# Two gated weight conversions more, a third fetch buffer and a second set of sum tiles in an attention plus two-MLP kernel

## The chip, the cores and the metric

The kernel runs on one core of a Trainium2 chip. The metric is the device time of one execution in microseconds (us), as the median of several runs.

## The reference

All data are float32; the weights reach the kernel as float64 and are narrowed on the chip.

```python
# attention: q, k, v of (4 batches, 12 heads, 448 rows, 64)
scores = cap * tanh((q @ k.T / 8) / cap)          # cap is 30
x = softmax(scores) @ v                           # heads side by side: 1792 x 768
h = x @ w_in                                      # first MLP, 768 x 2048
x = (h - tanh(h)) @ w_out                         # 2048 x 768
h = x @ w_in2                                     # second MLP, same shapes
out = (h * 1 / (1 + exp(-1.702 * h))) @ w_out2    # 1792 x 768
```

## The kernel before

The kernel runs in two phases. Attention goes through 24 groups `g` (a batch and a pair of heads). For each group TensorE makes transposes, scores and products with v; ScalarE (ACT) does tanh (L519) and exp (L521) on score tiles of 128x896; VectorE (DVE) does sums and copies. The order of these instructions is written by hand: `pin` keeps an instruction in program order on its engine. Everything that is not pinned is placed by a planner, which orders each engine's instructions by priority and by its own estimate of when their inputs are ready. Each engine then executes its list in the order so fixed.

The MLPs use TensorE with pairs of tiles: each operand is split in a rounded part and a rest (`hi_act` on ACT, L81; `lo_dve` on DVE, L93), and three products are added. The tokens are cut in two passes of 768 and 1024. The first layer's up projection (`gemm_in(0)`, product line L869) and its down projection for the first 768 tokens (`gemm_out`, L909) come first. Then come, for the 1024 tokens, `gemm_in(0)` again, the down projection in seven products instead of eight (`gemm_out_seven`, L962), the second up projection in seven products (`gemm_in_seven`, L1047) and the second down projection (`gemm_rows_seven`, L1149), and the last two again for the 768 tokens. `gemm_in_seven` makes 8 rounds `j` of 7 products, each 9 matmuls of 512 columns for the 1024 tokens.

Weights come in 64 chunks of 128x768. Chunks 0 to 15 are the first up projection, 16 to 31 the first down projection (A0 and up), 32 to 47 the second up projection (I0 and up), 48 to 63 the second down projection (R0 and up). A chunk is converted by `convert`: `conv_exp` on ACT (L193), `conv_low` on ACT (L200) or DVE (L202), `conv_or` on DVE (L208), and for chunks under 32 the split of L81 and L93. `conv_low` multiplies the low words in place in the landed tile `wd`; it needs nothing but the transfer. The transfer is issued by `dbl_dma` (L179) on the SP queue, called at the end of the `conv_or` of an earlier chunk. `wd` has two buffers (`wd_p`). A third (`some["wd"]`, opened at L1257 after attention in the program) is used where the running number of the transfer is divisible by three. `order` says which chunk has which number: nine "early" chunks (0, 1, 2, 4, 6, 8, 10, 12, 14) are numbers 0 to 8 and are converted inside the attention by hand; 3, 5, 7, 9, 11, 13, 15 are numbers 9 to 15, and `prepare` converts them in the loop of the first up projection. There `prepare` opens `tc.issue_after` for each instruction in `marks`: an instruction traced inside the block, if it is on the mark's engine, is placed behind the mark. `marks` holds the last exp of the attention (ACT) and the last reciprocal (DVE).

In the later stages, converted chunks lie in DRAM and `fetch` brings them back to `wr_p` (two buffers, tile `whole`), on the SP queue too; `third`, where it is not empty, is one more buffer for every third number, and makes `prepare` fetch two chunks ahead instead of one (L306). Side work runs beside the products: `sums_a`, `sums_i` (chunks 32 to 47) and `sums_b` (chunks 48 to 63, in four groups of four chunks, `group`) are generators, and `beside` takes a step of the first one each time that `due` has grown by one; it grows by `rate` at each call, which is once a chunk in the two seven-product stages concerned. `sums_b` takes six steps a group. `until("b")` ends it ahead of the second down projection.

Of the kernel before, what the change touches and what calls it, by code (L numbers as in the profile page):

```python
# [9 lines left out]
F32 = mybir.dt.float32  # L10
# [18 lines left out]
LEAD = 2  # L29
# [11 lines left out]
def attention_moe_moe(ctx, tc, q, k, v, cap, w_in1, w_out1, w_in2, w_out2, out):  # L41
# [3 lines left out]
    P = 128  # L45
# [6 lines left out]
    KF = DF // P  # L52
# [3 lines left out]
    WC = KM * P  # L56
    HW = DM // 2
    NT = max(TOKENS)
# [100 lines left out]
    early = [0, 1, 2, 4, 6, 8, 10, 12, 14]  # L159
    A0, I0, R0 = KF, 2 * KF, 3 * KF  # L160
    KQ = KF // 4
# [4 lines left out]
    n_raw, third, group, side_p, made = [0], [], [], [], [-1]  # L166
    n_dbl, n_ready, n_use = [0], [0], [0]
# [29 lines left out]
    def conv_low(i, act=False):  # L197
        low = dbls[i][:, :, 0]
        if act:
            pin(nc.scalar.mul(out=low, in_=low, mul=F64_LOW))  # L200
        else:
            pin(nc.vector.tensor_scalar(  # L202
                out=low, in0=dbls[i].bitcast(U16)[:, :, 1], scalar1=F64_LOW * 2.0 ** 16, scalar2=None, op0=ALU.mult
            ))
# [27 lines left out]

    def convert(i):
        conv_exp(i)
        conv_low(i, n_use[0] < KF or i >= I0)
        conv_or(i)
        if i < I0:
            conv_hi(i)
            conv_lo(i)
            n_ready[0] += 1  # L240

    KH = KF // 2
    SEVEN_A = ("11", "12", "s2", "s1", "s3", "s4", "22")
# [14 lines left out]
    W0 = len(stream)  # L258
# [25 lines left out]
    def prepare(upto):  # L284
        while n_ready[0] <= min(upto, len(stream) - 1):
            i = n_ready[0]
            if i < I0 and i not in early:
                with ExitStack() as behind:
                    if i < 2 * LEAD + 2:
                        for ins in marks:  # L290
                            behind.enter_context(tc.issue_after(ins))
                    convert(i)
                continue
            whl[i] = tuple(wh_p.tile([P, WC], F32R, tag=tag, name=tag) for tag in ("wh", "wl"))
            src, n, _ = stream[i]
            fetch(i)
            if i in whole:
                x = whole.pop(i)
                h, l = (t[:, :n] for t in whl[i])
                with tc.high_priority(offset=150):  # L300
                    hi_act(h, x)
                    lo_dve(l, x, h)
            else:
                for m, t in enumerate(whl[i]):
                    nc.sync.dma_start(out=t[:, :n].bitcast(F32), in_=src[:, m])
            for n in range(1, 2 + len(third)):  # L306
                fetch(i + n)
            n_ready[0] += 1
# [10 lines left out]
    side, due, rate = [], [0.0], [1.0]  # L319
# [18 lines left out]
    def add(out, a, kind, b):  # L338
        nc.vector.tensor_tensor(out=out, in0=a, in1=b, op=kind)
# [50 lines left out]

    def sums_b():
        for j in range(KQ):
            group[:] = [side_p[0].tile([P, WC], F32, tag="wr", name="group") for _ in range(2)]
            group.append(g_p.tile([P, NT], F32, tag="t", name="group")[:, :WC])
            group.extend(spare)
            for n in range(4):
                i = R0 + n * KQ + j
                convert(i)
                raws.pop(i)
                yield  # L400
            r11, r21, r12, r22 = group
            sub(r22, r22, r12)
            sub(r12, r12, r11)
            for m, t in (("t3", r22), ("t1", r12)):
                nc.sync.dma_start(out=side_b[m][j], in_=t)
            yield
            add(r11, r22, ALU.add, r11)
            sub(r21, r21, r11)
            for m, t in (("t2", r11), ("t4", r21)):
                nc.sync.dma_start(out=side_b[m][j], in_=t)  # L410
            yield
        done.add("b")
# [388 lines left out]
    gr, spare, ring, last_ts = [], [], [], []  # L801
# [134 lines left out]
    def gemm_out_seven():  # L936
        def three():
            return [one_bank("ps_y")[:, :HT] for _ in range(3)]

        def temps(*tags):  # L940
            return [part_of(t) for t in tags]

        LO, HI = slice(0, HT), slice(HT, NT)
        banks = {}
        p1 = u2 = None
        p5 = [gr[2 + e][:, HT:] for e in range(3)]
        for p, name in enumerate(SEVEN_A):
            rate[0] = .4 if p < 5 else 0.0
            head = {"12": "12", "s1": "s1", "s4": "s1"}.get(name, "11")
            if name == head:  # L950
                banks[head] = three()
            ps = banks[head]
            for j in range(KQ):
                i, (wh, wl) = w_next()
                ahead(i)
                for e in range(3):
                    c = slice(e * P, (e + 1) * P)
                    for kk in range(2):
                        k = 2 * j + kk
                        h, l = ring[k]  # L960
                        for m, (w, x) in enumerate(((wh, h), (wh, l), (wl, h))):
                            nc.tensor.matmul(  # L962
                                ps[e], w[:, kk, c], x,
                                start=(name == head and k == 0 and m == 0), stop=(k == KH - 1 and m == 2), skip_group_check=True,
                            )
                for k in (2 * j, 2 * j + 1):
                    if p < 6:
                        right(p + 1, k)
                    elif k in (3, 6):
                        for e in range(3):  # L970
                            split(ring[k - 3 + e], (p5 if k == 3 else u2)[e])
                if p == 0 and j == 0:
                    run_late()
            if p == 0:
                p1 = temps("far", "far", "v")
            elif p == 2:
                u2 = temps("q", "q", "t")
            with tc.high_priority(offset=AHEAD):
                for e in range(3):
                    if name == "11":  # L980
                        nc.scalar.copy(out=p1[e], in_=ps[e])
                    elif name == "12":
                        add(p1[e], ps[e], ALU.add, p1[e])
                    elif name == "s2":
                        nc.scalar.copy(out=u2[e], in_=ps[e])
                    elif name == "s1":
                        nc.scalar.copy(out=p5[e], in_=ps[e])
                    elif name == "s3":
                        add(p5[e], ps[e], ALU.add, p5[e])
                    elif name == "s4":  # L990
                        add(u2[e], ps[e], ALU.add, u2[e])
                    else:
                        x_out(3 + e, LO, ps[e])
            for e in range(3):
                if name == "12":
                    x_out(e, LO, p1[e])
                elif name == "s3":
                    x_out(3 + e, HI, p5[e])
                elif name == "s4":
                    sub(p1[e], u2[e], p1[e])  # L1000
                    x_out(e, HI, p1[e])
                    sub(u2[e], p5[e], u2[e])
                    sub(p5[e], p5[e], p1[e])
        t = g_p.tile([P, 2 * HT], F32R, tag="t", name="last_t")
        last_ts.append([ring[6], ring[7], [t[:, m * HT:(m + 1) * HT] for m in range(2)]])
        for e in range(3):
            sub(p5[e], ps[e], p5[e])
            split(last_ts[1][e], p5[e])

    def gemm_in_seven():  # L1010
# [14 lines left out]
        half_of = {"12": 1, "s4": 1, "s1": 1}  # L1025
        for j in range(KH):
            rate[0] = 1.0 if j else 0.0
            got, banks = {}, {}
            p1 = u2 = p5 = None
            for name in ("11", "s1", "s2", "12", "s3", "s4", "22"):  # L1030
# [180 lines left out]
    def moe():  # L1211
        yield from gemm_in(0)
        gemm_out()
        to_pass(1)
        plain[0] = True
        some.pop("stack").close()
        open_plain()
        side_p.append(end_of_x.enter_context(tc.tile_pool(name="side", bufs=2, side="right", reuse_waits="tile")))
        open_wide()
        side.append(sums_a())  # L1220
        side.append(sums_i(EARLY_I, KH))
        rate[0] = 1.3
        yield from gemm_in(0)
        run_late()
        until("a")
        open_banks(False)
        open_temps()
        third[:] = spare
        gemm_out_seven()
        third.clear()  # L1230
        side.append(sums_b())
        gemm_in_seven()
        until("b")
        gemm_rows_seven()
        to_pass(0)
        gemm_in_seven()
        gemm_rows_seven()
# [17 lines left out]
    g_p = pool("g", 2)  # L1255
# [43 lines left out]
```

## Time and profile before

| | us |
|---|---|
| median of 3 runs | 1080.12 |
| lowest, highest | 1079.32, 1080.51 |
| the profiled execution, its own time | 1077.66 |
| its span, first to last instruction | 1075.9 |
| PE busy (matmul) | 1055.8 |
| DVE busy | 808.1 |
| ACT busy | 706.8 |
| POOL busy | 53.7 |

PE is TensorE's matmul stream and PEld its weight loads. The mean granted TensorE clock of the execution is 0.995 of full speed. Busy time is summed over the span, so 20.1 us of the span show no matmul at all; matmuls are pipelined, and a wait between two of them can be hidden in the modelled end of the earlier one. In the timelines, the text in brackets is the idle time of the engine just before the instruction and what ended it.

### The profile page before, as it was taken

How to read it: one execution, taken by the hardware profiler on the slowest of the kernel's cores; microseconds unless marked ns; L12 is line 12 of the kernel's file. 1: busy time of each engine (PE TensorE's matmuls, PEld its weight loads, DVE VectorE, ACT ScalarE, POOL GpSimd, SP SyncE). 2: the span in 40 equal slices, each digit the busy share in tenths (PEclk: the TensorE clock that was granted, in tenths of full speed). 3: DMA queues.
4: the chain of work that ended last, by engine and by line, in shares of the span. 5: the costliest groups of instructions: out<-in, count | busy, mean ns of one | idle time of the engine just before them, and what ended most of it. 6: DMA issues, size and time to landing. Idle time of an engine off the chain costs nothing.

```text
span 1075.9 us, 15405 instructions
## 1 busy us (share of the span) xinstructions
PE 1055.8 (98%) x5483; PEld 861.0 (80%) x5483; DVE 808.1 (75%) x1073; ACT 706.8 (66%) x974; POOL 53.7 (5%) x56
## 2 busy tenths in 40 slices
PE   9799999999999999999999999999999999999998
PEld 3233333399999998888888887777799999999998
DVE  4467988799996553898999888656698883538973
ACT  6589889778783343567676676766655755657663
POOL 0012342400000000000000000000000000000000
PEclk9899999999999999999999999999999999999999
DMA  6665867665558899888765654888533554444443
GB/s 145 167 191 164 237 184 230 214 227 186 209 192 276 274 304 322 301 285 265 262 198 184 237 197 129 291 295 281 182 112 118 191 149 130 125 132 140 142 137 105
DMA packets 153749, 218.17 MB, mean 203 GB/s; under 512 B 58380, under 2 KB 101704, under 8 KB 153672
## 3 DMA queue, kind: packets, MB, share of 16 engines
q1 hardware_dynamic: 152376, 216.58, 63.6%
q8 instruction: 43, 0.70, 0.3%
q10 hardware_dynamic: 1296, 0.61, 0.2%
q14 instruction: 34, 0.28, 0.1%
HBM read 158.86 MB, written 58.28 MB: 202 GB/s over the span
## 4 chain that ended last, share of the span: by engine, by line
PE 90%; DMA 4%; ACT 2%; DVE 2%; issue 1%; SPq 1%; DVEq 0%; ACTq 0%
PE ps_h L869 22%; PE ps_o L1149 19%; PE ps_h L1047 12%; PE ps_y L962 11%; PE ps_y L909 9%; PE ps_pv L541 7%; PE ps_sc L500 5%; PE ps_qk L479 1%; DMA wd<-in_moe_w_out_dram 1%; DMA t<-group 1%; PE ps_tl L510 1%; PE ps_r L548 1%; DMA single<-spare 1%; PE ps_qk L488 1%; DVE wl L93 1%
## 5 line engine op out<-in xcount | busy, mean ns | idle before, releaser
L81 ACT CAST rh<-gr 128x512 fp32r<-128x512 f32 (+1 forms) x179 | 103.7, 584 | 101.9 <-PE ps_o L1149 70.8
L869 PE MATMUL ps_h<-x,wh 128*128 128x384 f32 (+1 forms) x672 | 152.9, 358 | 0.0
L93 DVE TENSOR_TENSOR rl<-gr,rh 128x512 fp32r<-128x512 f32 (+1 forms) x179 | 114.1, 642 | 36.9 <-ACT rh L81 36.2
L1149 PE MATMUL ps_o<-wh,rl 128*128 128x384 f32 x392 | 130.9, 334 | 0.0
L1149 PE MATMUL ps_o<-wh,rh 128*128 128x384 f32 x392 | 130.9, 334 | 0.0
L1149 PE MATMUL ps_o<-wl,rh 128*128 128x384 f32 x392 | 130.9, 334 | 0.0
L869 PEld LDWEIGHTS ps_h<-x,wh 128*128 128x128 f32 x672 | 121.1, 188 | 12.0 <-issue 0.7
L93 DVE TENSOR_TENSOR wl<-whole,wh 128x768 fp32r<-128x768 f32 (+1 forms) x113 | 103.0, 912 | 20.0 <-ACT wh L81 19.1
L81 ACT CAST wh<-whole 128x768 fp32r<-128x768 f32 (+1 forms) x113 | 90.4, 800 | 27.2 <-PE ps_h L1047 13.1
L1047 PE MATMUL ps_h<-x,wh 128*128 128x384 f32 (+1 forms) x336 | 97.3, 359 | 0.0
L869 PE MATMUL ps_h<-x,wl 128*128 128x384 f32 (+1 forms) x384 | 88.1, 364 | 0.0
L519 ACT ACTIVATE t<-ps_sc,tsc 128x896 f32<-128x896 f32 x72 | 70.0, 1005 | 23.1 <-PE ps_sc L500 23.1
L500 PE MATMUL ps_sc<-qk 64*128 64x448 f32 x288 | 69.3, 579 | 8.6 <-ACT t L519 7.8
L869 PEld LDWEIGHTS ps_h<-x,wl 128*128 128x128 f32 x384 | 69.8, 188 | 9.7 <-issue 1.4
L1149 PEld LDWEIGHTS ps_o<-wh,rh 128*128 128x128 f32 x392 | 73.6, 188 | 0.0
L1149 PEld LDWEIGHTS ps_o<-wl,rh 128*128 128x128 f32 x392 | 73.6, 188 | 0.0
L1149 PEld LDWEIGHTS ps_o<-wh,rl 128*128 128x128 f32 x392 | 73.6, 188 | 0.0
L521 ACT ACTIVATE t<-t,cpos 128x896 f32<-128x896 f32 x72 | 72.3, 1041 | 0.4
L1047 PE MATMUL ps_h<-x,wl 128*128 128x512 f32 (+1 forms) x192 | 69.6, 363 | 0.2 <-DVE wl L93 0.2
L193 ACT ACTIVATE wr<-wd 128x768 f32<-128x768 f32 x48 | 43.6, 910 | 36.3 <-DMA wd<-in_moe_w_out_dram 16.3
L541 PE MATMUL ps_pv<-t,rv 128*64 128x448 f32 x288 | 64.5, 554 | 2.6 <-ACT t L519 2.6
L1047 PEld LDWEIGHTS ps_h<-x,wh 128*128 128x128 f32 x336 | 61.7, 188 | 5.9
(144 smaller groups left out, 2163.6 us busy)
## 6 DMA issues: line engine op xcount, KB each, us to landing
wd<-in_moe_w_in_dram SPq DMA_DIRECT2D x64, 384.0 KB
wd<-in_moe_w_out_dram SPq DMA_DIRECT2D x32, 768.0 KB
whole<-s SPq DMA_DIRECT2D x40, 384.0 KB
whole<-single SPq DMA_DIRECT2D x39, 384.0 KB
wh<-kept SPq DMA_DIRECT2D x25, 384.0 KB
wl<-kept SPq DMA_DIRECT2D x25, 384.0 KB
single<-wr SPq DMA_DIRECT2D x24, 384.0 KB
whole<-t SPq DMA_DIRECT2D x22, 384.0 KB
```

The costliest lines, as they stand in the source:

```text
L81: pin(nc.scalar.copy(out=dst, in_=src))
L93: return pin(nc.vector.tensor_tensor(out=dst, in0=src, in1=hi.bitcast(F32), op=ALU.subtract))
L193: pin(nc.scalar.activation(out=raws[i][:, :width[i]], in_=dbls[i][:, :, 1].bitcast(F32), func=AF.Prelu, scale=2.0 ** -112, alpha=2.0 ** 32))
L500: pin(nc.tensor.matmul(ps[:, j, :S], qk[a, kc], qk[a, :S], start=True, stop=True))
L519: pin(nc.scalar.activation(out=t, in_=ps[:, :, :S], func=AF.Tanh, scale=tsc))
L521: ins = pin(nc.scalar.activation(out=tt[g, c], in_=tt[g, c], func=AF.Exp, scale=cpos))
L541: pin(nc.tensor.matmul(ps[a, :S], w, t[:, j], start=(c == 0), stop=(c == KC - 1)))
L869: pin(nc.tensor.matmul(ps, w[:, kk, :], x[kk][:, a], start=(m == 0), stop=(m == len(seq) - 1)))
L909: nc.tensor.matmul(bank[e][:, :a1 - a0], w[:, kk, c], x[2 * j + kk][:, a0:a1], start=(j == 0 and m == 0), stop=(j == KF // 2 - 1 and m == ...
L962: nc.tensor.matmul(ps[e], w[:, kk, c], x, start=(name == head and k == 0 and m == 0), stop=(k == KH - 1 and m == 2), skip_group_check=True,)
L1047: nc.tensor.matmul(ps, w, x, start=(name == head and m == 0), stop=(m == len(seq) - 1), skip_group_check=True,)
L1149: nc.tensor.matmul(ps[n], x[:, t], w[:, kk, :], start=(first and k == 0 and m == 0), stop=(k == KH - 1 and m == 2), skip_group_check=True,)
```

## The change

Six edits. The condition under which `conv_low` runs on ACT no longer takes in chunks 48 to 63: their sixteen go to DVE. The block of `issue_after` in `prepare` is opened for chunks under 12 instead of under 6, so that it holds the conversions of 3, 5, 7, 9 and 11 instead of 3 and 5. The second group of `sums_b` lives in four tiles `gr` that are free until round 5, instead of the side tiles, a tile of `g_p` and `spare`. The side rate in the first five products of `gemm_out_seven` is .6 instead of .4. In the `gemm_in_seven` of the 1024 tokens `fetch` gets a third buffer in `gr[15]`, until round 5 (there it is given up while side work remains; in the 768-token pass `third` stays `spare`).

```diff
     def convert(i):
         conv_exp(i)
-        conv_low(i, n_use[0] < KF or i >= I0)
+        conv_low(i, n_use[0] < KF or I0 <= i < R0)
         conv_or(i)
...
             if i < I0 and i not in early:
                 with ExitStack() as behind:
-                    if i < 2 * LEAD + 2:
+                    if i < len(early) + 3:
                         for ins in marks:
                             behind.enter_context(tc.issue_after(ins))
                     convert(i)
...
     def sums_b():
         for j in range(KQ):
-            group[:] = [side_p[0].tile([P, WC], F32, tag="wr", name="group") for _ in range(2)]
-            group.append(g_p.tile([P, NT], F32, tag="t", name="group")[:, :WC])
-            group.extend(spare)
+            if j == 1:
+                group[:] = [gr[f][:, :WC] for f in (KH + 5, KH + 6, KH - 2, KH - 1)]
+            else:
+                group[:] = [side_p[0].tile([P, WC], F32, tag="wr", name="group") for _ in range(2)]
+                group.append(g_p.tile([P, NT], F32, tag="t", name="group")[:, :WC])
+                group.extend(spare)
...
             yield
+            assert j != 1 or n_use[0] <= W0 + len(SEVEN_A) * KQ + 4 * (KH - 3)
             add(r11, r22, ALU.add, r11)
...
         for p, name in enumerate(SEVEN_A):
-            rate[0] = .4 if p < 5 else 0.0
+            rate[0] = .6 if p < 5 else 0.0
...
         for j in range(KH):
             rate[0] = 1.0 if j else 0.0
+            if j == KH - 3:
+                third[:] = [] if side else spare
...
         gemm_out_seven()
-        third.clear()
+        third[:] = [gr[2 * KH - 1][:, :WC]]
         side.append(sums_b())
         gemm_in_seven()
```

## Rows read from the trace of the kernel before

**Rows 1.** The page, first part: busy us, share of the span, instructions.

```profile
PE 1055.8 (98%) x5483; PEld 861.0 (80%) x5483; DVE 808.1 (75%) x1073; ACT 706.8 (66%) x974; POOL 53.7 (5%) x56
```

**Rows 2.** Busy us by stretch: length, engines, granted clock, DMA share, GB/s.

```profile
40.00:60.00 20.00, 14.53 (x70) 5.67 (x72) 6.36 (x8) 13.90 (x15) 2.65 (x2) 0.74 0.48 128
60.00:190.00 130.00, 129.84 (x725) 48.35 (x725) 110.76 (x134) 114.11 (x123) 37.01 (x30) 1.00 0.72 206
...
216.00:312.00 96.00, 96.00 (x556) 96.00 (x555) 89.30 (x101) 78.23 (x99) 0.00 (x0) 1.00 0.59 202
...
544.00:659.00 115.00, 115.00 (x508) 94.94 (x507) 107.49 (x161) 77.61 (x123) 0.00 (x0) 1.00 0.58 189
...
674.00:690.00 16.00, 15.12 (x66) 11.88 (x65) 11.75 (x16) 11.19 (x17) 0.00 (x0) 1.00 0.90 304
...
735.00:750.00 15.00, 14.19 (x62) 11.15 (x62) 8.31 (x11) 8.78 (x14) 0.00 (x0) 1.00 0.88 291
```

**Rows 3.** Waits of PE, whole span: us in total, times, longest.

```profile
PE ps_sc L500 <- ACT t L519: 7.8, 1, 7.8
```

**Rows 4.** Chain of waits in the attention: start us, us, what.

```profile
25.64 0.91 PE ps_tl L510 x8
...
38.80 4.74 DMA wd<-in_moe_w_in_dram
...
43.62 0.90 ACT wd L200
...
45.47 1.87 PE ps_sc L500 x4
...
52.17 0.91 PE ps_tl L510 x8
...
67.89 0.91 PE ps_tl L510 x8
```

**Rows 5.** Timeline of ACT around the stall and at the attention's end.

```profile
33.62 0.91 ACT L193 ACTIVATE wr<-wd 128x768 f32<-128x768 f32 x1
43.62 0.90 ACT L200 ACTIVATE wd<-wd 128x768 uint32<-128x768 uint32 x1 [9.10 <-DMA wd<-in_moe_w_in_dram]
...
215.18 0.49 ACT L759 ACTIVATE g_t<-ps_h 128x384 f32<-128x384 f32 x1 [2.99 <-PE ps_h L869]
```

**Rows 6.** Timeline of SP's issues in the attention.

```profile
26.22 0.47 SPq L179 DMA_DIRECT2D wd<-in_moe_w_in_dram  x1
...
27.39 1.13 SPq L179 DMA_DIRECT2D wd<-in_moe_w_in_dram  x2
...
38.16 1.13 SPq L179 DMA_DIRECT2D wd<-in_moe_w_in_dram  x2
...
57.09 0.91 SPq L179 DMA_DIRECT2D wd<-in_moe_w_in_dram  x2
```

**Rows 7.** Chain of waits, whole span, later stages.

```profile
543.83 114.54 PE ps_y L962 x504
...
754.89 25.31 PE ps_h L1047 x108
780.20 116.50 PE ps_o L1149 x672
```

**Rows 8.** Waits of PEld, then ACT, from 655 or 659 to 785 or 781.

```profile
PEld ps_h L1047 <- ACT part L1058: 4.2, 5, 1.2
...
ACT wh L81 <- DMA whole<-s: 8.2, 8, 2.4
...
ACT group L193 <- DMA t<-group: 4.7, 4, 1.9
```

**Rows 9.** Timeline of PEld in the stage's first round.

```profile
662.64 0.19 PEld L1047 LDWEIGHTS ps_h<-rh,wh 128*128 128x128 f32 x1 [0.62 <-ACT part L1058]
```

**Rows 10.** Groups by line: busy us, mean ns, idle before; ACT 659 to 781, then DVE whole.

```profile
L200 ACT ACTIVATE wd<-wd 128x768 uint32<-128x768 uint32 x12 | 10.8, 899 | 3.1 <-DMA wd<-in_moe_w_out_dram 3.0
...
L202 DVE TENSOR_SCALAR wd<-wd 128x768 uint32<-128x768 uint16 x24 | 13.5, 561 | 14.6 <-DMA wd<-in_moe_w_out_dram 14.6
```

## The prediction, made before the changed kernel ran

> **What bounds the kernel now.** I read the page's first part, then the busy time by stretch, the waits of PE, the chain of waits, and last the timelines of the places that these named. PE shows 98% of the span [rows 1], so only a few places are left in which a wait can go. The stretches show them: PE is full from 60 to 190 us and again in the projections, and has holes from 40 to 60 us, where the clock is down to 0.74 too, and in the second up projection for 1024 tokens, from 659 to 780 us [rows 2].
>
> The list of PE's waits names the first hole: one wait of 7.8 us for an ACT tanh [rows 3]. The chain says what that tanh waited for: a 0.90 us multiply on ACT (L200, `conv_low`) that itself waited for a weight transfer, 4.74 us to 43.54 [rows 4]. ACT stood idle 9.10 us before it [rows 5]. No hand-written conversion of the attention uses L200: the early ones call `conv_low` on DVE. So this is a conversion from the loop behind the attention that the planner put between two groups. Which one? Five pieces of `wd` transfer are issued in 26.22 to 39.3 us (the last piece of the first tile, then two pairs), the next pair only at 57.09 [rows 6]. So three `wd` tiles are in flight before any is given back, and one is in the third buffer. By `order`, the first number that gets it is 12, which is chunk 9. Its `conv_low` depends on nothing but its transfer, and 9 is not under 6, so no mark held it.
>
> **The change part by part.** All sums are made against the profiled execution's own 1077.66 us (span 1075.9, 1.8 around it); the median of the runs is 2.5 higher at 1080.12, and I carry the differences over to it.
>
> *The gate to 12.* It holds 7, 9 and 11 behind the last exp (ACT) and the last reciprocal (DVE); chunk 9 is the one that matters. The price of the stall comes from the spacing of the same step two groups apart: tail scores at 25.64, 52.17 and 67.89 [rows 4]. The disturbed pair of groups takes 52.17 - 25.64 = 26.53 us, the next one 67.89 - 52.17 = 15.72. The difference, 10.81 us, holds the wait, the 0.90 us multiply and the half-speed matmuls behind it (four scores took 1.87 us at 45.47). I take -10.8. The bound on the other side: the transfer itself is not gated (the mark acts on ACT and DVE, the issue is on SP), so its 768 KB still move at about 38 to 43.5 us in front of the q, k and v loads of later groups. If those came late instead, the stall would come back as a wait of PE, at most the same 10.8, so the term lies between 0 and -10.8. I go to the full end: the code asks for q and k one group ahead of their transposes (L655, L660), 15.72 / 2 = 7.9 us, against 4.74 us for the transfer in front of them, and the regular stretch runs with PE 129.84 of 130 us busy at the same kind of load, DMA share 0.72 [rows 2].
>
> What returns later: the 0.90 us multiply now stands behind the last exp. ACT waits 2.99 us for PE at 215.18 anyway [rows 5], and has 96 - 78.2 = 17.8 us idle in the first up projection, where PE is full [rows 2]. Chunk 9 is wanted six rounds after chunk 3, so its convert is not late. Cost 0; without that cover 0.9. Conversions 7 and 11 were behind the attention's end in this trace already, because their two buffers come free only when 3 and 5 are done: 0.
>
> *Third buffer, second set of tiles.* The stage's 504 matmuls begin where the L962 chain ends, 543.83 + 114.54 = 658.37, and end at 780.20: 121.8 us [rows 7]. The same count of 512-column matmuls took 114.5 us in L962. So 7.3 us is the most that can go here. The rate without waits is a little lower than L962's, though: the chain's last 108 took 25.31, or 0.234 each against 0.227, and 504 of them make 118.1. That leaves 3.7 us as the likely ceiling. The waits name the pattern: five times the weight loads wait for an ACT copy (L1058), 4.2 us in all, and ACT itself waits 8.2 us for late `whole` transfers and 4.7 us for group tiles whose store is not done [rows 8]; the copy stands in ACT's list behind them. The first of the five (0.62 us) is in round 0, before any of this [rows 9]. The other four make 3.6; a weight load normally runs one slot of 0.23 ahead of its matmul, so each is counted that much too long: 3.6 - 4 x 0.23 = 2.7 us. A fetch that starts a chunk earlier (the stage has 32, so 121.8 / 32 = 3.8 us each) exceeds the longest late landing, 2.4 us. The second set frees the group's first two conversions from the first group's stores. I take -2.7, with +2 and -7.3 as ends: the worse end is more transfers at once in a stretch that already runs at 0.88 to 0.90 DMA share and 291 to 304 GB/s [rows 2].
>
> The Trainium skill, in "DMA: Bandwidth & Descriptors", section Specifications, gives about 358 GB/s of HBM per core. By that, 304 GB/s leaves 15% and the earlier fetch has room, which is the sum above; by the DMA share of 0.90 of this trace there is 10% at best, and the sum without the stage's term is the first rival. No row tells the two apart, so the second reading has a rival's chance and not the forecast's.
>
> *`conv_low` of 48 to 63 on DVE.* Twelve L200 fall in the stage, 899 ns each, 10.8 us of ACT; on DVE the same work is 561 ns [rows 10], so 12 x 0.56 = 6.7 us go to DVE there and four more, 2.2 us, to the stage before. DVE is at 8.31 of 15 to 11.75 of 16 us in the stage [rows 2], so the busy time fits. ACT gets rid of work that sat ahead of its copies; I count that in the -2.7. The cost is a wait: DVE now stands behind a transfer at these places, with the splits that feed PE behind it. From the 24 such instructions of before: 14.6 us of idle time [rows 10]. Bounds 0 to 16 x 14.6 / 24 = 9.7 us if all of it reached PE. I take 0, since in those 24 PE stayed full, and keep the end for the rivals.
>
> *Rate .6.* 20 calls make 12 steps instead of 8, so that `sums_i` (two steps short before) ends inside `gemm_out_seven`, and `sums_b` starts two steps earlier. No instruction is added; two sums and two stores move. The stage before has DVE at 107.49 of 115 us and PE full [rows 2]: 7.5 us of DVE are free, against about 1.1 for the two sums and the 2.2 above. 0, and 3.3 if that cover is gone.
>
> Sum: -10.8 - 2.7 = -13.5 us. Own time 1064.2, and on the median's scale 1066.6 us.
>
> **The rivals.**
>
> *The stage gives nothing (1069.3).* The attention's stall goes, but transfers are the limit from 674 to 750 us, and an earlier fetch only moves the queue. For it: share 0.88 to 0.90. Against it: the stretch from 544 to 659 has 0.58, and the stage's end is lighter. 1080.1 - 10.8 = 1069.3.
>
> *The stall stays in another dress (1077.4).* The transfer of chunk 9 delays q and k loads, and PE waits for them instead of ACT for `wd`. For it: these loads and `wd` share SP's list, so what stands behind the issue at 38.16 comes later [rows 6]. Against: the lead of 7.9 us above. Only the stage's term is left: 1080.1 - 2.7 = 1077.4.
>
> *DVE's list blocks (up to 1095, slower).* One mechanism: each L202 of chunks 48 to 63 stands on DVE waiting for its transfer, with the split or the add that PE needs behind it. In rows 10 it is 14.6 us over 24. If, in the busier DMA of this stage, each of the sixteen waited 1.6 us and all reached PE, it would be +26: 1080.1 - 10.8 + 26 = 1095. It makes the kernel slower from 10.8 / 16 = 0.7 us a conversion on. Against: DVE is idle a quarter of the stage or more, and the average of the 24 is 0.6.
> The Trainium skill, in "TensorE: Matmul & The Clock Gate", section on the array's architecture, says that ACT's and DVE's lists are strictly first in, first out. The 9.10 us of ACT idle before L200 agree; by that rule the same trap is open on DVE.
>
> *Everything in the stage goes (1062.0).* 1080.1 - 10.8 - 7.3.
>
> **How the numbers follow.** Forecast 60% (its own range 1064 to 1069), nothing in the stage 25%, stall in another dress 6%, DVE blocks 4%, all of the stage 5%. The range 1063 to 1072 holds the first two with 2 us for a stage that gets a little worse, and leaves out the others. Under 0.2% (2.2 us) a measurement of this kernel can't be told from no change. Faster: the forecast, the first and the last rival, and half of the second, 93%; within 0.2% the other half, 3%; slower 4%.
>
> **What would show it.** Right: no L200 on ACT before about 209 us; tail scores 15.7 us apart from the start; the clock at 1.00 between 40 and 60; the stage from the last L962 to the first L1149 at 118 to 120 us instead of 121.8, with fewer waits for `whole`. Wrong: a wait of PE of several us in the attention for q, k or `wd`; waits of DVE L202 for `wd` next to waits of PE for `wl` in the stage; PE idle between 544 and 659.

## The result, and the profile after

The changed kernel takes 1068.57 us (median; 1067.26 to 1072.73, 4 runs) against 1079.72 (1079.27 to 1080.51, 4 runs): a ratio of 0.9903 [0.9874, 0.9931], 11.2 us less. Forecast were 1066.6 in 1063 to 1072. A second set of six runs, next to the experiments, gave 1067.72 against 1080.89, 0.9876 [0.9858, 0.9894]. The profile below is of an execution of 1072.73 us (span 1070.9), the longest of the first four. Lines up to L392 have kept their numbers; further down they moved by three to six (L500 is now L504, L962 is L966, L1047 is L1053, L1149 is L1155).

First the page's engine line, against [rows 1], and the busy time by stretch (length, PE, PEld, DVE, ACT, POOL, granted clock, DMA share, GB/s), against [rows 2]; the later stretches are shifted with the work.

```profile
PE 1053.8 (98%) x5483; PEld 859.2 (80%) x5483; DVE 815.1 (76%) x1089; ACT 692.5 (65%) x958; POOL 53.8 (5%) x56
```
```profile
40.00:60.00 20.00, 20.00 (x114) 7.15 (x112) 14.69 (x18) 18.27 (x20) 2.65 (x2) 1.00 0.84 229
60.00:190.00 130.00, 128.65 (x720) 47.19 (x716) 111.40 (x132) 114.86 (x124) 45.54 (x39) 1.00 0.72 208
201.00:300.00 99.00, 99.00 (x574) 97.86 (x573) 89.78 (x102) 78.40 (x100) 0.00 (x0) 1.00 0.58 198
534.00:653.00 119.00, 115.97 (x503) 93.27 (x502) 111.08 (x165) 76.24 (x119) 0.00 (x0) 1.00 0.59 192
669.00:685.00 16.00, 16.00 (x71) 13.12 (x70) 13.51 (x19) 10.22 (x17) 0.00 (x0) 1.00 0.91 304
730.00:745.00 15.00, 14.92 (x65) 11.94 (x64) 8.32 (x12) 8.81 (x14) 0.00 (x0) 1.00 0.71 238
```

PE is full from 40 to 60 us and the clock stays at 1.00 (2.4 GHz), where it was 0.74 before. ACT has 16 instructions fewer (974 to 958) and DVE 16 more: the `conv_low` of 48 to 63. The stretch before the second up projection, 534 to 653, has lost PE time that it did not lose before; more on that below.

PE's waits up to the end of the attention (us in total, times, longest), against [rows 3], and the tail scores in the chain of waits, against [rows 4]:

```profile
PE ps_pv L545 <- ACT t L523: 2.5, 3, 1.2
...
PE ps_sc L504 <- ACT qk L81: 0.6, 1, 0.6
```
```profile
24.89 0.91 PE ps_tl L514 x8
...
40.61 0.91 PE ps_tl L514 x8
...
56.33 0.91 PE ps_tl L514 x8
...
72.04 0.91 PE ps_tl L514 x8
```

The 7.8 us wait is gone, and the tail scores stand 15.72 us apart from the first on. The timeline of ACT at the attention's end, against [rows 5], and SP's issues of `wd`, against [rows 6]:

```profile
198.10 0.93 ACT L200 ACTIVATE wd<-wd 128x768 uint32<-128x768 uint32 x1
...
203.61 0.49 ACT L763 ACTIVATE g_t<-ps_h 128x384 f32<-128x384 f32 x1 [2.19 <-PE ps_h L873]
```
```profile
27.92 1.13 SPq L179 DMA_DIRECT2D wd<-in_moe_w_in_dram  x2
37.53 1.12 SPq L179 DMA_DIRECT2D wd<-in_moe_w_in_dram  x2
48.78 0.94 SPq L179 DMA_DIRECT2D wd<-in_moe_w_in_dram  x2
```

The first multiply on ACT now stands behind the last exp, and ACT still waits 2.19 us for PE after it. The transfer is issued as early as before (37.53 against 38.16): only the multiply has moved. That the first L200 stands at 198.10 and not at the 209 of the prediction's sign is the same gain once more: the 209 was read from the kernel before, where the attention ends later.

The later stages in the chain, against [rows 7], and the waits of PE (two lines), then DVE and ACT, in the second up projection for 1024 tokens (653 to 776 us), against [rows 8]:

```profile
401.74 132.10 PE ps_h L873 x576
533.84 12.25 PE ps_y L966 x54
...
775.71 116.50 PE ps_o L1155 x672
```
```profile
PE ps_h L1053 <- DVE part L339: 3.3, 2, 2.3
PE ps_h L1053 <- ACT part L1064: 0.7, 1, 0.7
...
DVE wd L202 <- DMA wd<-in_moe_w_out_dram: 16.2, 7, 5.1
...
ACT wh L81 <- DMA whole<-s: 5.2, 2, 4.1
```

[rows 8] has the waits of PEld. PE's own list for that stage in the kernel before (655 to 785 us) begins:

```profile
PE ps_h L1047 <- ACT part L1058: 2.1, 5, 0.8
```

The chain no longer runs through L966 as one piece. Measured from first matmul to first matmul, this stage takes 119.76 us in this execution (114.53 before), and the one behind it 122.11 (121.84 before). In the latter, of PE's five waits for the ACT copy at L1058 (now L1064) one is left, 0.7 us instead of 2.1; ACT's wait for stores of group tiles is down from 4.7 us to 0.3 and the one for `whole` from 8.2 to 5.2; and a new wait is there: DVE for `wd`, 16.2 us over 12 instructions, against [rows 10]:

```profile
L202 DVE TENSOR_SCALAR wd<-wd 128x768 uint32<-128x768 uint16 x12 | 6.7, 559 | 16.2 <-DMA wd<-in_moe_w_out_dram 16.2
```

How it reaches PE stands in the timelines of DVE and PE at one place:

```profile
694.43 0.57 DVE L202 TENSOR_SCALAR wd<-wd 128x768 uint32<-128x768 uint16 x1 [3.27 <-DMA wd<-in_moe_w_out_dram]
695.46 0.96 DVE L208 SCALAR_TENSOR_TENSOR group<-group,wd 128x768 uint32<-128x768 uint32 x1 [0.46 <-ACT group L193]
...
698.27 0.95 DVE L93 TENSOR_TENSOR wl<-whole,wh 128x768 fp32r<-128x768 f32 x1
699.14 1.28 DVE L339 TENSOR_TENSOR part<-ps_h,part 128x512 f32<-128x512 f32 x2
```
```profile
696.96 0.63 PE L1053 MATMUL ps_h<-x,wh 128*128 128x512 f32 x2
699.88 0.50 PE L1053 MATMUL ps_h<-rh,wh 128*128 128x512 f32 x1 [2.29 <-DVE part L339]
```

DVE stands 3.27 us in front of a `wd` that isn't there; the adds that empty PE's banks are behind it in the list, and 3 us later PE has no bank to write to. The Trainium skill, "TensorE: Matmul & The Clock Gate", section on the array's architecture, calls ACT's and DVE's lists strictly first in, first out; these rows agree, with the 3.27 us.

### The profile page after: what moved, and what is told of

It is laid out like the page before. It is cut to its first block, busy times and chain, and to the rows that moved or that the text cites. A ratio compares the mean times of both kernels' runs of the same rounds, so it can differ in the third digit from the quotient of the medians.

```text
span 1070.9 us, 15396 instructions
## 1 busy us (share of the span) xinstructions
PE 1053.8 (98%) x5483; PEld 859.2 (80%) x5483; DVE 815.1 (76%) x1089; ACT 692.5 (65%) x958; POOL 53.8 (5%) x56
## 4 chain that ended last, share of the span: by engine, by line
PE 73%; DVE 11%; DMA 9%; ACT 3%; issue 3%; SPq 1%; DVEq 0%; ACTq 0%
PE ps_h L873 19%; PE ps_o L1155 19%; PE ps_h L1053 12%; PE ps_pv L545 7%; PE ps_sc L504 5%; DMA wd<-in_moe_w_out_dram 5%; PE ps_y L913 4%; DVE wl L93 3%; DVE rl L93 2%; DVE gr L339 1%; PE ps_y L966 1%; PE ps_qk L483 1%; PE ps_tl L514 1%; PE ps_r L552 1%; DVE part L339 1%
## 5 line engine op out<-in xcount | busy, mean ns | idle before, releaser
L1155 PE MATMUL ps_o<-wl,rh 128*128 128x384 f32 x392 | 130.9, 334 | 0.0
L1155 PE MATMUL ps_o<-wh,rl 128*128 128x384 f32 x392 | 130.9, 334 | 0.0
L1155 PE MATMUL ps_o<-wh,rh 128*128 128x384 f32 x392 | 130.9, 334 | 0.0
L93 DVE TENSOR_TENSOR wl<-whole,wh 128x768 fp32r<-128x768 f32 (+1 forms) x102 | 92.8, 910 | 17.4 <-ACT wh L81 16.6
L1053 PE MATMUL ps_h<-x,wh 128*128 128x384 f32 (+1 forms) x336 | 97.5, 359 | 0.2 <-ACT wh L81 0.2
L81 ACT CAST wh<-whole 128x768 fp32r<-128x768 f32 (+1 forms) x102 | 81.4, 799 | 22.1 <-PE ps_h L1053 12.2
L1155 PEld LDWEIGHTS ps_o<-wh,rh 128*128 128x128 f32 x392 | 73.6, 188 | 0.0
L1155 PEld LDWEIGHTS ps_o<-wl,rh 128*128 128x128 f32 x392 | 73.6, 188 | 0.0
L1155 PEld LDWEIGHTS ps_o<-wh,rl 128*128 128x128 f32 x392 | 73.6, 188 | 0.0
L1053 PE MATMUL ps_h<-x,wl 128*128 128x512 f32 (+1 forms) x192 | 69.6, 363 | 0.3 <-DVE wl L93 0.3
L504 PE MATMUL ps_sc<-qk 64*128 64x448 f32 x288 | 67.9, 570 | 0.8 <-ACT qk L81 0.6
L966 PE MATMUL ps_y<-rh,wl 128*128 128x512 f32 x168 | 66.1, 393 | 2.6 <-DVE wl L93 2.6
L1053 PEld LDWEIGHTS ps_h<-x,wh 128*128 128x128 f32 x336 | 61.6, 188 | 6.4 <-ACT wh L81 0.6
```

Source lines behind the costliest of these rows:

```text
L81: pin(nc.scalar.copy(out=dst, in_=src))
L93: return pin(nc.vector.tensor_tensor(out=dst, in0=src, in1=hi.bitcast(F32), op=ALU.subtract))
L504: pin(nc.tensor.matmul(ps[:, j, :S], qk[a, kc], qk[a, :S], start=True, stop=True))
L966: nc.tensor.matmul(ps[e], w[:, kk, c], x, start=(name == head and k == 0 and m == 0), stop=(k == KH - 1 and m == 2), skip_group_check=True,)
L1053: nc.tensor.matmul(ps, w, x, start=(name == head and m == 0), stop=(m == len(seq) - 1), skip_group_check=True,)
L1155: nc.tensor.matmul(ps[n], x[:, t], w[:, kk, :], start=(first and k == 0 and m == 0), stop=(k == KH - 1 and m == 2), skip_group_check=True,)
```

## The experiments

My theory: all of the gain that can be measured is chunk 9's multiply, which no longer stands on ACT between two groups; the edits to the second up projection trade one wait for another and come to nothing. After the first profile these questions were open, and the expectations name them by letters. Why does the stage of L962 take 5.2 us more in the profile of after: because everything behind the attention comes earlier (A), because of the rate or another edit (B), or because DVE waits some 15 us for a `pair` of quarters at about 415 us and has its side work behind it (C)? And why does the second up projection gain nothing: because `conv_low` on DVE waits for its transfers (D), or because transfers are the limit and a third buffer can't help (E)? The stage lengths given are of one profiled execution each; two executions with the same order of instructions on every engine differ by 0.3 to 1.4 us in the second up projection and by up to 3.6 in the stage of L962.

**The gate alone**, in the kernel before:

```
-                    if i < 2 * LEAD + 2:
+                    if i < len(early) + 3:
```

> The kernel before with the gate's edit alone (chunks under 12 behind the marks), nothing else. Both theories: tail scores 15.7 us apart from the start, and the attention ends 11.6 us earlier than before (300.2 instead of 311.7 us for the first matmul of L909). Theory A, lag: the transfers and VectorE behind them do not get earlier by as much as TensorE does, so VectorE reaches the seven-product down projection later beside TensorE than before, and that stage takes 117 to 120 us instead of 114.5; time 1070 to 1072. Theory B: the stage was made longer by the other edits (rate .6 and conv_low on VectorE); without them it takes 114.5 us and the time is 1068.2.

1071.19 us (1066.12 to 1074.66), ratio 0.9921 [0.9895, 0.9946]. The stall is gone. So most of the gain is this one number. In the two traces the order of instructions differs in one place: the L200 that is the 29th of ACT's instructions before is the 186th here, and PE, PEld, DVE, POOL and SP keep their order.

**Everything but the gate**: the changed kernel with that line set back.

> The changed kernel without the gate (chunks under 6 again). The stall of some 10.8 us in the attention is back. Theory A: the seven-product down projection is at 114.5 us as before, and the second up projection at its changed length of 122; time 1077 to 1080. Theory B: that down projection takes 119 us; time 1082 to 1085.

1078.86 us (1075.37 to 1080.58, 12 runs), ratio 0.9985 [0.9965, 1.0004]. The second up projection takes 121.58 us, as in the kernel before (121.84), and the stage of L962 119.02. So the other edits together are worth between 3.8 us and -0.4, and A falls: the longer L962 stage is there without the gate.

**Gate and rate**, in the kernel before (`rate[0] = .6` beside the gate):

> The kernel before with the gate and the side rate .6, no other edit. Against the gate alone it tells what the rate costs. Theory A: the seven-product down projection and the time are those of the gate alone within 1 us. Theory B with the rate as cause: 2 to 5 us slower than the gate alone, in that stage.

1070.27 us (1067.12 to 1073.41), ratio 0.9925 [0.9904, 0.9946]; L962 117.74, second up projection 122.47. No difference from the gate alone.

**Which chunk.** The gate to 12 holds three conversions more than before, 7, 9 and 11 (the title has two). The gate to 8, which holds 7 and not 9 or 11:

```
-                    if i < 2 * LEAD + 2:
+                    if i < 8:
```

> The kernel before with the gate for chunks under 8, so that 3, 5 and 7 are held and 9 is not. If chunk 9 in the third buffer is what stalls the attention, as the prediction has it: nothing changes, one multiply on ScalarE with some 9 us of idle time ahead of it near 43 us, time 1079 to 1081. If it was chunk 7: the stall is gone and the time 1068 to 1071.

1079.23 us (1074.08 to 1084.83), ratio 1.0001 [0.9976, 1.0026]. The timeline of ACT and the busy time by stretch of this kernel show the stall as it was:

```profile
43.80 0.88 ACT L200 ACTIVATE wd<-wd 128x768 uint32<-128x768 uint32 x1 [10.21 <-DMA wd<-in_moe_w_in_dram]
```
```profile
40.00:60.00 20.00, 14.38 (x74) 5.66 (x76) 7.46 (x10) 14.97 (x17) 2.65 (x2) 0.78 0.53 142
```

It is not 7. As built, this kernel has every engine's instructions in the same order as the kernel before, so it is also a second look at that kernel, and there the L962 stage took 118.11 us: the 114.53 of [rows 7] were a favourable execution. B falls with it as the cause of all 5.2 us.

Then 9 alone beside the old marks, with the rate .6; 7 and 11 are free:

```
-                    if i < 2 * LEAD + 2:
+                    if i < 2 * LEAD + 2 or i == 9:
```

> The kernel before with the mark on chunk 9 alone beyond the old ones (3 and 5), and the rate .6; neither 7 nor 11 is held, conv_low of 48 to 63 stays on ACT, there is no third buffer and no second set of tiles. If chunk 9 alone made the stall: no L200 on ACT before the attention's end, tail scores 15.7 us apart from the first on, and the time of the run with the whole gate and the rate, 1070.3 (ratio 0.9925). If 11 made it (or takes its place): an ACT multiply with about 10 us of idle time ahead of it between two groups, and about 1079. As the cell of a two by two table (buffers and tiles: no; conv_low on DVE: no) it is the base that the three others are compared with.

1069.16 us (1065.63 to 1072.34), ratio 0.9897 [0.9873, 0.9921]. Its stretch and its first multiply on ACT:

```profile
40.00:60.00 20.00, 20.00 (x114) 7.16 (x114) 14.65 (x18) 18.29 (x21) 2.65 (x2) 1.00 0.81 224
```
```profile
198.33 0.94 ACT L200 ACTIVATE wd<-wd 128x768 uint32<-128x768 uint32 x1
```

Chunk 9 alone makes the stall, and marks on 7 and 11 add nothing: this kernel has the same order of instructions on every engine as the one with the whole gate and the rate.

**The second up projection, two by two.** On one chip, next to the kernel just shown (neither edit), ran the gate and the rate with `conv_low` of 48 to 63 on DVE alone, the changed kernel, and the changed kernel with that `conv_low` back on ACT (third buffer and second set of tiles alone). The one line that moves it:

```
-        conv_low(i, n_use[0] < KF or i >= I0)
+        conv_low(i, n_use[0] < KF or I0 <= i < R0)
```

> The kernel before with the gate to 12 and the rate .6 and conv_low of 48 to 63 on DVE; no third buffer, no second set of tiles. Theory D (the wait of DVE for these transfers costs something in any case): 1 to 1.5 us over the base cell, 1071.5. The rival (it costs only because the third buffer starts transfers earlier and both collide): no more than the base, 1070.3 or, by the run without the third buffer, 1069.8.

> The changed kernel as it is, beside the three others on one chip. If the two by two table adds up (buffers and tiles about -3, conv_low on DVE about +1.4): 1068.6. If the difference between it and the kernel with conv_low on ACT came from different chips: both at the same time within 1 us.

> The changed kernel with conv_low of 48 to 63 on ACT, as before the change: the cell with buffers and tiles alone. By the earlier run 1067.2, 1.4 under the changed kernel and 3.1 under the base cell, which would be the -2.7 that the prediction gave the stage. If the earlier run was luck: 1068 to 1069, like the changed kernel.

| gate, rate and | us (runs) | ratio to before | 2nd up projection | its PE waits |
|---|---|---|---|---|
| nothing else | 1069.16 (6) | 0.9897 [0.9873, 0.9921] | 121.08 | 3.1 |
| `conv_low` on DVE | 1068.04 (5) | 0.9878 [0.9860, 0.9897] | 119.63 | 2.3 |
| buffers and tiles | 1067.56 (6) | 0.9884 [0.9865, 0.9902] | 120.89 | 2.3 |
| both: the change | 1067.72 (6) | 0.9876 [0.9858, 0.9894] | 122.42 | 4.2 |

The times can't be told apart, and the four stage lengths span 2.8 us where executions of one order differ by up to 1.4. The waits can be told apart. (The upper two kernels have the line numbers of the kernel before.) PE's and DVE's waits in the stage, in the kernel with `conv_low` on DVE alone:

```profile
PE ps_h L1047 <- DVE part L339: 1.1, 1, 1.1
...
DVE wd L202 <- DMA wd<-in_moe_w_out_dram: 8.1, 5, 3.6
```

In the changed kernel of the same table:

```profile
PE ps_h L1053 <- DVE part L339: 3.6, 2, 2.5
...
DVE wd L202 <- DMA wd<-in_moe_w_out_dram: 14.8, 7, 5.2
```

PE's and ACT's waits in the one with buffers and tiles alone:

```profile
PE ps_h L1053 <- ACT part L1070: 1.8, 1, 1.8
```
```profile
ACT wh L81 <- DMA whole<-s: 1.3, 2, 0.7
```

And ACT's wait in the one with neither:

```profile
ACT wh L81 <- DMA whole<-s: 8.9, 7, 2.2
```

So the third buffer does what it is for: ACT's wait for `whole` goes from 8.9 to 1.3 us, and E falls as far as a late fetch goes. The stage gets no shorter by it: one wait for another ACT copy, 1.8 us for L1070 (L1064 before), stands in the list of PE where the four for L1058 stood. D is half right: there is a wait of DVE in any case, 8.1 us, and PE waits 1.1 us for DVE's adds at L339, 3.6 with both edits, against 0 to 0.3 in the seven profiles with `conv_low` on ACT and no other ordering. But the stage is not shorter without it, as D had it.

The edits get in each other's way: with both, DVE's wait for `wd` grows to 14.8 us. It is not the third buffer that makes it grow. The kernel without that buffer, further down, has the tiles and `conv_low` on DVE, and there DVE waits nearly as long (649 to 773 us):

```profile
DVE wd L202 <- DMA wd<-in_moe_w_out_dram: 13.7, 6, 5.3
```

What these kernels share is the second set of tiles. The traces also show a difference in the twelve `wd` transfers that are issued in the stage, from issue to the last of their semaphore updates: on average 5.4 to 5.8 us in the six profiles without the second set, and 6.1 to 6.5 in the eight with it. They don't start later: on average 45.6 us into the stage with `conv_low` on DVE alone, 44.2 to 44.6 in the changed kernel. Why they take longer was not taken apart; the tiles were not tried alone.

Two runs from before that table, on the same chip, belong to it. **The changed kernel with `conv_low` on ACT**, a first time:

> The changed kernel with conv_low of chunks 48 to 63 back on ScalarE; gate, third buffer, second set of tiles and rate as changed. Theory D: in the second up projection the edits took away the waits for the ACT copy, and the moved conv_low gave the time back, since VectorE stands at L202 until a transfer lands. Then the waits for VectorE's adds (3.3 us of TensorE in the changed kernel) go and the stage takes 118 to 120 us instead of 122; time 2 to 3 us under the changed kernel, 1066. Theory E: the transfers themselves are the limit of the stage, so something else waits and the stage stays at 121 to 122.

1067.18 us (1066.29 to 1068.74), ratio 0.9886 [0.9858, 0.9913]. The stage took 122.14 us, so the 118 to 120 of D did not come; one wait of PE for L1070, 2.3 us, is the longest in it. **The changed kernel without the third buffer**, the tiles and `conv_low` on DVE kept:

```
-            if j == KH - 3:
-                third[:] = [] if side else spare
...
-        third[:] = [gr[2 * KH - 1][:, :WC]]
+        third.clear()
```

> The changed kernel without the third fetch buffer in the second up projection (cleared ahead of it as before). If the buffer is worth what it was predicted to be: ScalarE waits for late whole transfers again (8 us in all), and the stage gets 2 us longer, 124. If it is worth nothing beside the moved conv_low: 121 to 123 us, time as the changed kernel, 1068 to 1070.

1069.82 us (1068.72 to 1072.0), ratio 0.9912 [0.9886, 0.9938], stage 123.85 us. Its ACT waits for `whole` again:

```profile
ACT wh L81 <- DMA whole<-s: 10.9, 11, 2.2
```

These two looked like a gain of 1.4 us from ACT and one of 1.3 from the buffer; in the table, on one chip, the first is 0.2.

**The wait for `pair` (C).** The changed kernel with each of `sums_a`'s first sums marked to come behind the newest masked copy of the gate, so that DVE doesn't stand waiting for a `pair`:

```
-            for m, t in first_sums(*r):
+            sums = first_sums(*r)
+            for _ in range(4):
+                with tc.issue_after(last_q[0].ins):
+                    m, t = next(sums)
...
-            nc.vector.copy_predicated(out=q, mask=m.bitcast(U16), data=far)
+            last_q[:] = [nc.vector.copy_predicated(out=q, mask=m.bitcast(U16), data=far)]
```

> The changed kernel with one more ordering edge: each of the first sums of sums_a stands behind the newest finished activation of the first up projection on VectorE, so that VectorE no longer stands at the first of them, waiting some 15 us for a load, while an activation is ready. Theory C: that wait runs 3.6 to 4.9 us past the point at which the first activation is ready, makes VectorE late for the whole stage, and comes out as 3 to 5 us of TensorE's waits in the seven-product down projection (117.7 to 119.8 us in five of six profiles). Then that stage takes 114.5 us, and the time is 1064 to 1066. Rival: VectorE is late there because of its total work (over 90% busy); then the stage stays at 118 to 120 us and the time at 1068 to 1071.

1074.81 us (1071.99 to 1080.29, 12 runs), ratio 0.9958 [0.9938, 0.9979]: about 6 us slower than the changed kernel. With `conv_low` on ACT as well:

> The ordering edge of the kernel just above and conv_low of chunks 48 to 63 on ScalarE together. Theories C and D both right: seven-product down projection 114.5 us, second up projection 118 to 120 us, time 1061 to 1063. Only C: 1064 to 1066. Neither: 1068 to 1070.

1076.85 us (1074.99 to 1083.32, 12 runs), ratio 0.9976 [0.9957, 0.9994]. No expectation came in either run: both are slower than all of them. The profile of the first of the two is of its longest run (1080.29 us), and its lines stand three further down than those of the changed kernel. DVE's waits in it between 398 and 531 us:

```profile
DVE g_far L767 <- ACT g_t L766: 13.6, 5, 10.3
DVE pair L339 <- DMA pair<-single: 5.7, 2, 4.2
```

and, in the changed kernel of the table (400 to 532 us):

```profile
DVE pair L339 <- DMA pair<-single: 17.5, 4, 14.0
```

The wait for `pair` shrank, and as much idle time came up at another place. What seems to have paid for it are the sums behind. In that stage and the next, 531 to 783 us, DVE does 18 sums of `wr`:

```profile
L339 DVE TENSOR_TENSOR wr<-wr 128x384 f32<-128x384 f32 x18 | 10.0, 558 | 4.4 <-DMA single<-wr 4.2
```

and 12 in the changed kernel, 532 to 774:

```profile
L339 DVE TENSOR_TENSOR wr<-wr 128x384 f32<-128x384 f32 x12 | 6.7, 556 | 0.1
```

The L962 stage took 123.76 us and the second up projection 128.34 (120.77 and 126.43 in the other run's profile). PE's waits in both stages of the slower kernel:

```profile
PE ps_h L1056 <- ACT part L1067: 4.6, 2, 3.0
PE ps_y L969 <- ACT wh L81: 4.3, 1, 4.3
```

Two stretches of the changed kernel, the one with the wait and the first half of the L962 stage, point to why:

```profile
400.00:466.00 66.00, 66.00 (x290) 54.09 (x289) 46.89 (x45) 34.55 (x37) 0.00 (x0) 1.00 0.84 296
...
532.00:592.00 60.00, 57.97 (x251) 46.30 (x250) 58.91 (x85) 40.04 (x60) 0.00 (x0) 1.00 0.57 178
```

C falls as I tried it: the 14 us lie where PE is full and cost nothing there, while work pushed behind them lands where DVE is busy 58.91 of 60 us. That the six sums alone make the 6 us is argued from these rows; no run moved them back.

## Why the prediction was right, and where a term was off

*The gate.* Right in mechanism, place and size. The first matmul of L909, at the end of the first up projection behind the attention, comes at 311.73, 310.63 and 310.50 us in the three profiles with the stall, and between 298.65 and 300.42 in ten of the eleven without it. The means, 310.95 and 299.51, are 11.4 us apart, against the 10.8 that I had from the spacing of the tail scores. By times, the kernels with the gate and none of the stage's edits are 8.6, 9.5 and 11.7 us faster than the kernel before on their chips. Chunk 9 as the culprit is shown by the kernels that add a mark on 7 alone and on 9 alone, and the multiply as the cause by the gate alone, which moves no other instruction. The half-speed matmuls that the term counted are gone too: four scores took 1.87 us at 45.47 [rows 4], and in the changed kernel seven take 1.77 us at 43.86. The bound at 0, q and k late instead, did not come true in the changed kernel: no wait of PE for a load is in its list. The eleventh profile, of the gate alone, does have late q and k loads, its L909 starting at 302.78; that is one execution.

*The multiply later: 0.* Right. ACT has 2.19 us idle behind it, and PE has 99.00 of 99 us in the projection.

*Third buffer and second set of tiles: -2.7.* This is the term that was too large as the change stands. The waits that it was read from went: `whole` 8.9 to 1.3 us when buffers and tiles come alone. But the stage is 121.6 to 122.4 us in three profiles with all three edits and 120.5 to 122.6 in five without buffers, tiles or the moved `conv_low`: 0 within what executions differ by. With buffers and tiles alone it is 120.89 and 122.14. The step that failed is the one that took the four waits for L1058 as the whole of it and assumed that nothing would take their place. With `conv_low` on DVE, which I priced apart, DVE's wait does, 3.3 and 3.6 us of PE; with `conv_low` on ACT one wait for L1070 does, 1.8 and 2.3 us. The size was generous as well: the waits were read from PEld, 4.2 us for five, where PE's own list has 2.1 for the same five.

*`conv_low` on DVE: 0, bounds 0 and 9.7.* The value within what can be measured, for a reason that was half right. I argued that PE had stayed full in the 24 such waits of before. In the stage it does not: 3.3 and 3.6 us of PE in two profiles of the changed kernel. The idle time of an L202 there, 16.2 / 12 = 1.35 us, is near the 1.6 that the slower rival assumed; its other half, that all of it reaches PE, was wrong: 3.3 of 16.2 does. That its gain on ACT makes up for this is argued and not shown: by the table, PE's waits go from 3.1 to 2.3 us without the buffers, and from 2.3 to 4.2 with them. In the L962 stage, to which four of the sixteen went, five profiles with it have 118.3 to 119.8 us and seven without it 114.5 to 119.1, means 119.2 and 117.3 (the two with the sums moved are left out). The times of the table (1068.04 against 1069.16, and 1067.72 against 1067.56) don't show such a cost, so I leave it open.

*Rate: 0.* Nothing contradicts it: 1070.27 with it against 1071.19 without.

*The sum.* -10.8 and 0 give 1069.3, the first rival in its time, but only partly for its reason: earlier fetches did land, where that rival had transfers as the limit; on the other hand each `wd` transfer took longer. With buffers and tiles taken at -2.7 it is 1066.6. The measured 1068.57 and 1067.72 lie between, and the times alone can't choose. The profiles choose: the gain is in the attention. That the forecast came within 2 us does not confirm the -2.7. On bandwidth, the Trainium skill ("DMA: Bandwidth & Descriptors", Specifications) gives about 358 GB/s for a core, which would leave some 15% at 304 GB/s, an estimate from that figure. No run shows this room used: the busiest of the stretches shown moves 304 GB/s before and after the change, at a DMA share of 0.90 and 0.91.

*The signs.* Those for the attention came: tail scores 15.72 us apart and a clock of 1.00. The one for the second up projection, 118 to 120 us, did not: it takes 122.11. Two that were to tell of a wrong prediction came in small: PE idle in the stage of L962 (115.97 of 119 us busy), which the kernel before has as well in another execution (118.11 us instead of 114.53), and waits of DVE for `wd` in the second up projection, with PE behind them at L339 and only 0.3 us at `wl`.

*A fault in the base.* 114.5 us for L962 [rows 7] stood as the length that a stage of 504 matmuls can reach. The kernel with the same order of instructions on every engine took 118.11 in another execution, so the ceiling of 7.3 rested on one lucky stage.

No version beat the changed kernel by more than can be measured; marking chunk 9 alone, with the rate, gets within 1.4 us of it.

## What to carry to other kernels

When an engine's list is laid out by a planner, look in the trace for an instruction of side work that sat idle for a transfer between two instructions of the main loop: its price is the spacing of a regular step with and without it, and it can be one instruction of nine hundred. Before paying for a wait, see whether PE is idle in that stretch; moving a wait that costs nothing can push work to where it costs something. And take a stage's length from more than one execution before calling the difference of two stages a ceiling.

## What the runs showed of the hardware that was not expected

The same order of instructions gave 114.53 and 118.11 us in one stage, at a granted clock of 1.00 in both; PE's waits in the second hold this line, and those of the first are empty:

```profile
PE ps_y L962 <- DVE wl L93: 1.9, 2, 1.6
```

DVE is busy 93% of that stretch before (107.49 of 115) [rows 2]. What made it late in the second execution stays open: its longest wait for a transfer there is 2.2 us, and 2.1 in the first. Whole runs of the kernel before went from 1074.8 to 1086.0 us in 23 executions, so edits worth under 2 us were not to be separated with 5 or 6 runs each.
